# A decode step of attention and MLP: queries that wait in PSUM, a weight ring with four places, one batch's K scored inside another's softmax

## The chip, the cores and the metric

The kernel runs on one core of a Trainium2 chip. The metric is the device time of one execution in microseconds. A core has engines that run side by side: TensorE (PE in the profile, with its weight loads as PEld), VectorE (DVE), ScalarE (ACT), GpSimd (POOL) and SyncE (SP), which here issues nearly all DMA transfers. 16 DMA engines move the data from HBM to SBUF, the memory of 128 partitions on which the engines work; PSUM is the memory in which matmuls accumulate.

## The reference

Two identical layers are applied to one token of each of 8 batches, all in float32. Each layer is attention with a cache of 4096 keys, and then an MLP:

```python
def _A_ref(x, k_cache, v_cache, wq, wo):      # x: 8 x 1 x 1024
    q = (x @ wq)                              # 32 heads of 128
    k, v = each of the 4 cached heads serves 8 query heads   # 8 x 4 x 4096 x 128
    p = softmax(q . k * 128**-0.5)
    return (p . v) @ wo                       # 4096 -> 1024
def _B_ref(x, w1, b1, w2, b2):
    return gelu(x @ w1 + b1) @ w2 + b2        # 1024 -> 3584 -> 1024

x = x + _A_ref(_layernorm(x), ...)
x = x + _B_ref(_layernorm(x), ...)
x = x + _A_ref(_layernorm(x), ...)            # the same caches and weights again
x = x + _B_ref(_layernorm(x), ...)
return x
```

K and V of one batch are 8.39 MB each. Both layers read the same caches and weights.

## The kernel before

**Space.** Nearly all of SBUF is one tile, `arena`, of 216 units of 1 KB a partition. Regions A, B (named `Bb`) and C hold 64 units each, which is one batch's K or V; C's last 8 units are the first place of a ring of four places `R[0]` to `R[3]` (units 184 to 215), each for a weight tile of 1 MB. The queries of all batches (`qz`, 3 units at 200) lie in the ring's third place; the row of scores (4 units at 208) and the transposed probabilities `S` (4 units at 212) fill the fourth. So the ring has all four places only while these are not in use.

**Order of transfers.** A list `stream` holds every load in the order in which it is to be issued. `pump` issues from its head as long as the head's place is free; `give` frees a place in program order and calls `pump`. The issue itself sits in SyncE's queue and waits there until the last reader of the place is done. SyncE is in order: a load that waits holds up all behind it. The program order is written out by hand; engines run their own queues in that order.

**A layer.** `layernorm` transposes x on TensorE, subtracts the mean with further matmuls, and leaves the standard deviation to a function `variance` that is put on the list `pending`; `flush` empties that list, and is called after each step of `expand` (x times wq or w1, in two halves u = 0, 1 with eight steps each) and `project` (times wo or w2). Also the end of a half of `expand` goes to `pending`: `query_unit(u)` transposes that half's queries and copies them into `qz`, whose other columns must be zero (`open_queries` clears it on GpSimd).

**Attention.** For each batch the 8 K tiles (4 heads times 2 halves of the keys) are multiplied with the queries (`scores`), the softmax's maximum and exponential follow (`probs`), the probabilities are transposed (`turn`), and the 8 V tiles are multiplied (`values`); the end of each head pair's sum is done by `heads` a little later. A K or V tile's place is given back after its last reader.

**Between the layers.** Layer 0 goes through batches 0 to 7, layer 1 from 7 down to 0. K and V of batch 7 and K of batch 6 stay in SBUF from layer 0 to layer 1; the last tile of K of batch 6 lies in `R[0]` and is parked in PSUM meanwhile (`park`, `unpark`), so that the ring can run. The weights wo, w1, w2 of layer 0 and wq of layer 1 pass through the ring, 1 MB at a time: each tile can be loaded when the tile four before it has been multiplied. At the end of half 0 of layer 1's queries, `qz` is opened, which takes the third place out of the ring; the second half uses `R[0]`, `R[1]`, `R[3]` and the first place of region B, where K of batch 7 lies and must be scored first. That is why four K tiles of batch 7 are scored early (`early`), each behind one step of the second half. Then come, in `stream`, V of batch 6 in four pieces of 2 MB into region B, K of batch 5 in halves into region A (where V of batch 7 lies until it is multiplied) and V of batch 5 into region C. From then on each K or V of a batch is one transfer of 8.39 MB.

## Time and profile before

| | us |
|---|---|
| median of 3 runs | 881.45 (880.26 to 885.93) |
| the profiled execution | 881.5 |
| its span | 879.7 |

| in the profiled execution | |
|---|---|
| PE busy | 546.7 us, 62% of the span |
| PE weight loads | 182.9 us |
| DVE busy | 181.6 us |
| ACT busy | 47.4 us |
| read from HBM | 369.28 MB, 420 GB/s over the span |
| mean granted clock of TensorE | 0.79 |

The profile shows one execution; its times are counted from the start of the span. Layer 0's attention lasts until about 359 us, its MLP until about 468, layer 1's queries until about 513, its attention until about 781 and the rest to 877. Matmuls in float32 are recorded as two records each, so that a tile of four matmuls shows as eight. The page's share of busy time is a mean over these stages; what holds a stage up is read from that stage's own rows. In a table of stretches each row gives start and end, length, busy time of PE, weight loads, DVE, ACT and POOL with the number of instructions, the granted clock, the mean share in which the DMA engines were busy and the GB/s moved, counted where packets end.

### The profile page before, as it was taken

The numbers are of one execution on the slowest core, as the hardware profiler recorded it, in microseconds if no ns is written. First come the engines' busy times: TensorE is split into PE (matmuls) and PEld (weight loads), VectorE is DVE, ScalarE is ACT, GpSimd is POOL, SyncE is SP. The second block draws the span as 40 slices with busy tenths as digits, with TensorE's granted clock in tenths as the row PEclk, the third lists the DMA queues.
The fourth block names the chain that finished last, engine by engine and source line by source line (L and its number), as shares of the span: only waits on it lengthen the run. The fifth ranks groups of instructions, "written<-read, shape, count | busy, mean of one in ns | idle before, by whom it ended". The sixth has DMA issues, their size and how long they took to land.

```text
span 879.7 us, 8979 instructions
## 1 busy us (share of the span) xinstructions
PE 546.7 (62%) x3984; PEld 182.9 (21%) x3984; DVE 181.6 (21%) x585; ACT 47.4 (5%) x75; POOL 2.4 (0%) x13
## 2 busy tenths in 40 slices
PE   0556575555756567767667666776765655654665
PEld 0212121221212122223222122222121211222222
DVE  0002232312123232201100023333221313120110
ACT  0200000000000010000000010000000000000000
POOL 0000000000000000000000000000000000000000
PEclk9977787877777877777877879778787777777889
DMA  9999999999999999999999998999999999999997
GB/s 387 446 416 454 444 427 427 427 432 430 435 436 430 433 416 424 409 419 396 419 418 408 388 392 352 443 458 427 424 429 430 430 438 433 432 436 416 440 424 298
DMA packets 16519, 369.99 MB, mean 421 GB/s; under 512 B 1984, under 2 KB 2272, under 8 KB 2400
## 3 DMA queue, kind: packets, MB, share of 16 engines
q1 hardware_dynamic: 16336, 369.28, 98.5%
q8 instruction: 31, 0.51, 0.2%
q10 hardware_dynamic: 144, 0.13, 0.0%
q14 instruction: 8, 0.07, 0.0%
HBM read 369.28 MB, written 0.13 MB: 420 GB/s over the span
## 4 chain that ended last, share of the span: by engine, by line
DMA 68%; PE 24%; DVE 6%; issue 1%; ACT 1%; ACTq 0%; DVEq 0%; SPq 0%
DMA arena<-in_A_v_cache_dram 27%; DMA arena<-in_B_w_dram 16%; DMA arena<-in_A_k_cache_dram 16%; PE o_ps L336 7%; PE sps L280 7%; PE acc L190 4%; DMA arena<-in_A_wo_dram 4%; DMA arena<-in_A_wq_dram 3%; DVE scratch L344 3%; DMA x_row<-in_A_x_dram 3%; PE y L249 2%; PE sps L351 1%; DVE scratch L342 1%; PE sps L314 1%; DVE arena L287 1%
## 5 line engine op out<-in xcount | busy, mean ns | idle before, releaser
L280 PE MATMUL sps<-arena 128*32 128x512 f32 x992 | 140.2, 701 | 87.4 <-DMA arena<-in_A_k_cache_dram 74.0
L336 PE MATMUL o_ps<-arena 128*32 128x512 f32 x1024 | 156.8, 742 | 7.5 <-DMA arena<-in_A_v_cache_dram 7.4
L249 PE MATMUL y<-arena,oT 128*32 128x256 f32 x960 | 79.4, 477 | 53.0 <-DMA arena<-in_A_wo_dram 31.5
L190 PE MATMUL acc<-arena,xnT 128*32 128x512 f32 (+3 forms) x528 | 83.4, 716 | 44.2 <-DMA arena<-in_B_w_dram 24.0
L344 DVE SCALAR_TENSOR_TENSOR scratch<-o_ps,misc,scratch 128x128 f32<-128x128 f32 x192 | 67.3, 351 | 6.8
L280 PEld LDWEIGHTS sps<-arena 128*32 128x32 f32 x992 | 31.1, 124 | 172.8 <-DMA arena<-in_A_k_cache_dram 74.7
L314 PE MATMUL sps<-ident,arena 128*128 128x128 f32 x128 | 31.7, 393 | 43.3 <-ACT arena L303 31.4
L249 PEld LDWEIGHTS y<-arena,oT 128*32 128x32 f32 x960 | 32.0, 130 | 99.0 <-DMA arena<-in_A_wo_dram 34.6
L351 PE MATMUL sps<-misc,scratch 128*128 128x8 f32 x128 | 27.5, 288 | 33.7 <-DVE scratch L344 33.7
L287 DVE TENSOR_SCALAR_CACHE_REDUCE arena<-sps 128x512 f32<-128x512 f32 x31 | 21.4, 691 | 121.7 <-PE sps L280 121.7
L303 ACT ACTIVATE arena<-arena,bias 128x1024 f32<-128x1024 f32 x16 | 18.4, 1147 | 521.9 <-DVE scratch L300 521.9
L336 PEld LDWEIGHTS o_ps<-arena 128*32 128x32 f32 x1024 | 31.5, 129 | 70.8 <-issue 60.5
L351 PEld LDWEIGHTS sps<-misc,scratch 128*128 128x128 f32 x128 | 21.7, 213 | 105.1 <-DVE scratch L344 87.3
L342 DVE TENSOR_SCALAR scratch<-o_ps,misc 128x128 f32<-128x128 f32 x64 | 22.5, 351 | 98.2 <-PE o_ps L336 98.2
L190 PEld LDWEIGHTS acc<-arena,xnT 128*32 128x32 f32 x528 | 19.8, 127 | 92.4 <-DMA arena<-in_A_wq_dram 36.8
L353 DVE TENSOR_TENSOR oT<-sps,scratch 128x8 f32<-128x8 f32 x64 | 11.1, 173 | 111.1 <-PE sps L351 111.1
L314 PEld LDWEIGHTS sps<-ident,arena 128*128 128x128 f32 x128 | 20.2, 195 | 51.4 <-ACT arena L303 34.5
L258 DVE SCALAR_TENSOR_TENSOR x_row<-y,x_row 128x256 f32<-128x256 f32 x4 | 1.7, 425 | 110.1 <-PE y L249 110.1
L205 DVE TENSOR_SCALAR scratch<-acc,rs 128x512 f32<-128x512 f32 (+1 forms) x8 | 5.5, 684 | 81.9 <-PE acc L190 81.9
L296 PE MATMUL sps<-scratch,misc 128*128 128x128 f32 x32 | 7.8, 325 | 21.4 <-DVE scratch L292 21.4
L133 PE MATMUL sps<-ident,x_row 128*128 128x32 f32 x16 | 4.5, 373 | 25.0 <-DMA x_row<-in_A_x_dram 23.3
L319 DVE COPY arena<-sps 128x512 f32<-128x512 f32 x16 | 11.1, 691 | 40.6 <-PE sps L314 40.6
(68 smaller groups left out, 137.4 us busy)
## 6 DMA issues: line engine op xcount, KB each, us to landing
arena<-in_B_w_dram SPq DMA_DIRECT2D x29, 1024.0 KB, 8.4
arena<-in_A_wo_dram SPq DMA_DIRECT2D x16, 1024.0 KB, 8.5
arena<-in_A_wq_dram SPq DMA_DIRECT2D x16, 1024.0 KB, 8.7
arena<-in_B_w_dram SPq DMA_DIRECT2D x2, 7168.0 KB
arena<-in_A_k_cache_dram SPq DMA_DIRECT2D x3, 4096.0 KB
arena<-in_A_v_cache_dram SPq DMA_DIRECT2D x3, 4096.0 KB, 25.1
arena<-in_A_v_cache_dram SPq DMA_DIRECT2D x5, 2048.0 KB, 11.9
arena<-in_B_w_dram SPq DMA_DIRECT2D x1, 5120.0 KB
```

Of the source, the lines that this page charges most:

```text
L190: nc.tensor.matmul(acc[32 * j:32 * j + 32, lo - begins[j]:hi - begins[j]], xnT[:, kt * B:kt * B + 32], arena[:, base * KB + c + lo - a:bas ...
L249: nc.tensor.matmul(y[32 * j:32 * j + 32, 0:Q4], lhs[:, kt * B:kt * B + 32], arena[:, e:e + Q4], start=(kt == 0), stop=(kt == n_k - 1))
L280: nc.tensor.matmul(ps[32 * g:32 * g + 32, :], qz[:, c:c + 32], kt[:, g * CH:(g + 1) * CH], start=(j == 0), stop=(j == HKV - 1))
L287: nc.vector.tensor_scalar(row[:, half * CH:(half + 1) * CH], ps, SCALE, None, op0=ALU.mult, op1=ALU.max, accum_out=st["mx"][:, half:half + 1])
L303: nc.scalar.activation(row, row, AF.Exp, bias=bias, scale=1.0, accum_out=ls)
L314: nc.tensor.transpose(pp[:, t * P:(t + 1) * P], row[:, c:c + P], ident)
L319: nc.vector.tensor_copy(s[:, half], src)
L336: nc.tensor.matmul(o[32 * g:32 * g + 32, :], s[:, g], v[:, g * CH:(g + 1) * CH], start=(half == 0), stop=(half == NH - 1))
L342: nc.vector.tensor_scalar(r, o[:, 0:P], sel_t[:, 0:1], None, op0=ALU.mult)
L344: nc.vector.scalar_tensor_tensor(r, o[:, t * P:(t + 1) * P], sel_t[:, t:t + 1], r, op0=ALU.mult, op1=ALU.add)
L351: nc.tensor.matmul(po[:, 0:REP], scratch[:, a:a + DH], sel_h, start=True, stop=True)
L353: nc.vector.tensor_tensor(oT_v[:, j * REP:(j + 1) * REP, b], po[:, 0:REP], scratch[:, a + j * REP:a + (j + 1) * REP], ALU.mult)
```

## The change

It has four parts, all between layer 0's MLP and layer 1's attention but for the first.

- `layernorm` subtracts the mean with one matmul ahead of the two transposes in place of one behind each. `variance` and the other pending work are done after the second ring tile, no longer after the first (for the second half of an `expand` after the first 2048 columns, in `project` after four steps).
- The queries of half 0 of layer 1 are transposed after the first tile of half 1 and stay in PSUM; only those of batch 7 are copied, into the start of `oT` (`q7`, cleared on GpSimd after tile 3 of half 0). The early scores of batch 7 read them there. `qz` is opened and filled behind tile 6 of half 1 (tiles are counted from 0), so wq's second half uses all four ring places. The parked tile returns behind tile 4 of half 1.
- In layer 1 K of batch 6 is scored within the softmax of batch 7 (`ahead=6`): two tiles ahead of `probs`, two behind it, and four behind `turn`. Its row of scores takes a second place (`AT_ROW2`), and its first half accumulates in the pool of two buffers.
- K of batch 5 is loaded to region C, where K of batch 6 lies, and V of batch 5 to region A; the later homes swap A and C accordingly, and the pieces of layer 1's w2 lie in A and B.

```diff
-AT_QZ, AT_ROW, AT_S = 200, 208, 212
+AT_QZ, AT_ROW, AT_S, AT_ROW2 = 200, 208, 212, 203
...
     def layernorm(xr, rsum):
         pt = small_ps("pt")
+        nc.tensor.matmul(pt[:, 0:8 * B], rsum.to_broadcast([P, P]), nmean[:, 0:B].unsqueeze(1).to_broadcast([P, 8, B]), start=True, stop=False)
         for i in range(2):
-            o = pt[:, i * 4 * B:(i + 1) * 4 * B]
-            nc.tensor.matmul(o, xr[:, i * P:(i + 1) * P], ident.rearrange("p (j q) -> p j q", j=4)[:, :, 0:B], start=True, stop=False)
-            nc.tensor.matmul(o, rsum.to_broadcast([P, P]), nmean[:, 0:B].unsqueeze(1).to_broadcast([P, 4, B]), start=False, stop=True)
+            nc.tensor.matmul(pt[:, i * 4 * B:(i + 1) * 4 * B], xr[:, i * P:(i + 1) * P],
+                             ident.rearrange("p (j q) -> p j q", j=4)[:, :, 0:B], start=False, stop=(i == 1))
...
-                    flush()
+                    if at >= (2 - u) * W:
+                        flush()
...
+    q7 = oT[:, 0:Q_AT[1] + PAD]
+
+    def query_unit_late(u):
+        src = turned(2 * REP)
+        if u == 1:
+            put_queries(1, src)
+            return
+        for e in range(2):
+            nc.vector.tensor_copy(q7[:, Q_AT[e]:Q_AT[e] + REP], src[:, e * REP:(e + 1) * REP, B - 1])
+        st["q0"] = src
+
+    def open_queries_late():
+        open_queries()
+        put_queries(0, st.pop("q0"))
...
-                flush()
+                if kt >= 4:
+                    flush()
...
+        for b in order:
+            score(b)
+            nxt = ahead if b == order[0] else None
+            if nxt is not None:
+                score(nxt, 2)
             probs(b)
+            if nxt is not None:
+                score(nxt, 2)
             turn(b)
+            if nxt is not None:
+                score(nxt)
...
-    weights("q1", wq, [ring[0:8], [(e, TILE) for e in (R[0], R[1], R[3], Bb) * 2]])
-    cache(1, v_keys(6), vc[6], [(Bb + 32, 2), (Bb, 2), (Bb + 16, 2), (Bb + 48, 2)])
-    cache(1, k_keys(5), kc[5], [(A, 4), (A + 32, 4)])
-    cache(1, v_keys(5), vc[5], [(C, 4), (C + 32, 4)])
+    weights("q1", wq, [ring[0:8], ring[0:8]])
+    cache(1, v_keys(6), vc[6], [(Bb, 2), (Bb + 32, 2), (Bb + 16, 2), (Bb + 48, 2)])
+    cache(1, k_keys(5), kc[5], [(C, 4), (C + 32, 4)])
+    cache(1, v_keys(5), vc[5], [(A, 4), (A + 32, 4)])
...
-    weights("p1", w2, [[(C, 40), (C + 40, 28), (C + 68, 20), (Bb, 12), (Bb + 12, 8), (Bb + 20, 4)]])
+    weights("p1", w2, [[(A, 40), (A + 40, 28), (A + 68, 20), (A + 88, 12), (A + 100, 8), (A + 108, 4)]])
...
     def early(key):
-        scores(key, spare=key[3] == 1)
+        scores(key, spare=key[3] == 1, late=True)
         give(pieces[key], TILE)
...
-            expand("q1", W, rs, query_unit, {(0, "end"): open_queries} | {(1, i): (lambda key=key: early(key)) for i, key in enumerate(first)})
+            expand("q1", W, rs, query_unit_late, {(0, 3): clear, (1, 4): unpark, (1, 6): open_queries_late}
+                   | {(1, i): (lambda key=key: early(key)) for i, key in zip((1, 2, 3, 5), first)})
             flush()
-            last = attention(range(B)[::-1], set(), done=first, after={7: unpark})
+            last = attention(range(B)[::-1], set(), done=first, ahead=6)
```

How the rows stand in TensorE's queue, from the end of layer 0 on. Before, the start of layer 1 (L133 and L134 transpose x and subtract the mean, L127 spreads a sum, L190 are the tiles of wq, L217 transposes queries, L280 scores a K tile with four rows):

```order
L133 MATMUL sps<-ident,x_row 128x32
L134 MATMUL sps<-nmean,rsum 128x32
L133 MATMUL sps<-ident,x_row 128x32
L134 MATMUL sps<-nmean,rsum 128x32
L127 MATMUL sps<-rsum,nmean 32x1 x4
L190 MATMUL acc<-arena,xnT 32x512 x4
L127 MATMUL sps<-ss,nmean 32x1 x4
L190 MATMUL acc<-arena,xnT 32x512 x32
L217 MATMUL sps<-ident,scratch 128x128 x4
L280 MATMUL sps<-arena 32x512 x4
L190 MATMUL acc<-arena,xnT 32x512 x4
L280 MATMUL sps<-arena 32x512 x4
```

The same place in the changed kernel (the lines are now L134, L132, L128, L191, L219 and L301):

```order
L132 MATMUL sps<-nmean,rsum 128x64
L134 MATMUL sps<-ident,x_row 128x32 x2
L128 MATMUL sps<-rsum,nmean 32x1 x4
L191 MATMUL acc<-arena,xnT 32x512 x8
L128 MATMUL sps<-ss,nmean 32x1 x4
L191 MATMUL acc<-arena,xnT 32x512 x28
L219 MATMUL sps<-ident,scratch 128x128 x4
L191 MATMUL acc<-arena,xnT 32x512 x4
L301 MATMUL sps<-arena,oT 32x512 x4
L191 MATMUL acc<-arena,xnT 32x512 x4
L301 MATMUL sps<-arena,oT 32x512 x4
```

One matmul fewer stands ahead of the first tile, the variance stands behind two tiles instead of one, and the first early score behind the second tile of half 1 instead of the first, reading its queries from `oT`.

Before, from the last query transposes to the first V tiles of batch 7 (L296 is the maximum's matmul, L314 turns the probabilities, L321 their sum, L336 a V tile's rows):

```order
L217 MATMUL sps<-ident,scratch 128x128 x4
L280 MATMUL sps<-arena 32x512 x8
L280 MATMUL s_ps<-arena 32x512 x8
L296 MATMUL sps<-scratch,misc 128x128
L314 MATMUL sps<-ident,arena 128x128 x8
L321 MATMUL sps<-scratch,misc 128x32
L336 MATMUL o_ps<-arena 32x512 x12
```

And in the changed kernel (L318, L336, L343 and L358 for these):

```order
L219 MATMUL sps<-ident,scratch 128x128 x4
L301 MATMUL sps<-arena 32x512 x8
L301 MATMUL s_ps<-arena 32x512 x16
L318 MATMUL sps<-scratch,misc 128x128
L301 MATMUL s_ps<-arena 32x512 x8
L336 MATMUL sps<-ident,arena 128x128 x8
L343 MATMUL sps<-scratch,misc 128x32
L301 MATMUL sps<-arena 32x512 x16
L358 MATMUL o_ps<-arena 32x512 x12
```

The 32 rows of batch 6's K, which came behind batch 7's V, now stand in three groups around batch 7's softmax; the V tiles of batch 7 come behind all of them. SyncE's queue holds the same transfers in the same order as before, into other places.

More of the change, by code (lines that the diff above doesn't have):

```diff
@@ L111, in open_queries @@
         nc.gpsimd.memset(qz, 0.0)
+    st = {}
     pending = []
@@ L301, in probs @@
         ls = small.tile([P, 1], F32, name="ls")
-        row = place(AT_ROW, 4)
+        row = place(rows[b], 4)
         nc.scalar.activation(row, row, AF.Exp, bias=bias, scale=1.0, accum_out=ls)
@@ L306, in turn @@
     def turn(b):
-        row = place(AT_ROW, 4)
+        row = place(rows[b], 4)
         take(AT_S, 4, "S")
@@ L354, in heads, with attention, score @@
                                 scratch[:, a + j * REP:a + (j + 1) * REP], ALU.mult)
-    def attention(order, keep, done=(), after={}):
-        for b in order:
-            for key in k_keys(b):
-                if key in done:
-                    continue
-                scores(key)
+    def attention(order, keep, done=(), after={}, ahead=None):
+        scored = set(done)
+        def score(b, n=NR):
+            for key in [e for e in k_keys(b) if e not in scored][:n]:
+                scored.add(key)
+                scores(key, spare=b == ahead and key[3] == 0)
                 while ready:
```

33 lines of the change are left out of this document (19 added, 14 removed).

## The prediction

> **What bounds the kernel now.** I read the page's slices in time and its DMA part first, then the chain of waits, then tables of stretches, then the SyncE queue's issues.
>
> ```profile
> DMA  9999999999999999999999998999999999999997
> GB/s 387 446 416 454 444 427 427 427 432 430 435 436 430 433 416 424 409 419 396 419 418 408 388 392 352 443 458 427 424 429 430 430 438 433 432 436 416 440 424 298
> q1 hardware_dynamic: 16336, 369.28, 98.5%
> DMA 68%; PE 24%; DVE 6%; issue 1%; ACT 1%; ACTq 0%; DVEq 0%; SPq 0%
> ```
>
> The DMA engines are busy nearly everywhere and the chain that ended last is 68% DMA. So the time is 369.28 MB over the rate, plus the stretches in which the engines starve. The GB/s digits dip in slices 23 to 25 (22 us each). The table of stretches shows where; its last three columns are granted clock, DMA share and GB/s.
>
> ```profile
> 398.00:412.00 14.00, 10.42 (x74) 4.79 (x74) 0.97 (x4) 2.14 (x4) 0.00 (x0) 0.73 0.96 379
> 412.00:466.00 54.00, 36.11 (x310) 12.18 (x310) 4.81 (x16) 1.88 (x3) 0.00 (x0) 0.78 1.01 419
> 473.00:482.00 9.00, 6.07 (x48) 1.11 (x44) 0.16 (x1) 0.62 (x2) 0.00 (x0) 0.77 1.00 391
> 490.00:496.00 6.00, 4.44 (x38) 1.24 (x30) 0.47 (x2) 0.00 (x0) 0.00 (x0) 0.94 0.82 287
> 512.00:515.00 3.00, 2.27 (x20) 0.96 (x24) 0.73 (x3) 0.00 (x0) 0.00 (x0) 1.00 0.88 300
> 516.00:528.00 12.00, 7.21 (x40) 2.84 (x36) 4.07 (x13) 2.75 (x4) 0.00 (x0) 0.73 1.02 406
> 528.00:534.00 6.00, 4.54 (x40) 1.50 (x36) 3.16 (x10) 0.00 (x0) 0.00 (x0) 0.97 0.39 128
> 545.00:600.00 55.00, 39.52 (x264) 13.48 (x260) 19.14 (x62) 3.67 (x6) 0.00 (x0) 0.81 1.01 437
> 600.00:860.00 260.00, 159.08 (x1224) 56.38 (x1216) 55.80 (x182) 13.21 (x22) 0.00 (x0) 0.78 1.00 432
> ```
>
> Three full rates can be read: 419 with the ring's 1 MB tiles, 406 with V of batch 6 (2 MB pieces, share 1.02), 432 with K and V in larger pieces. Against them five stretches fall short: 398 to 412, 473 to 482, 490 to 496, 512 to 515 and 528 to 534. From 545 to 860 the DMA never lacks work, so a microsecond of transfer won before 545 is a microsecond at the end, as long as no new gap opens.
>
> Who holds the transfers back? SyncE issues in order; these are its issues around the gaps (start, duration, what).
>
> ```profile
> 482.96 0.33 SPq L163 DMA_DIRECT2D arena<-in_A_wq_dram  x1
> 488.80 0.33 SPq L163 DMA_DIRECT2D arena<-in_A_wq_dram  x1
> 493.31 0.33 SPq L163 DMA_DIRECT2D arena<-in_A_wq_dram  x1
> 501.43 0.33 SPq L163 DMA_DIRECT2D arena<-in_A_v_cache_dram  x1
> 511.50 0.33 SPq L163 DMA_DIRECT2D arena<-in_A_v_cache_dram  x1
> 517.09 0.33 SPq L163 DMA_DIRECT2D arena<-in_A_v_cache_dram  x1
> 531.33 0.33 SPq L163 DMA_DIRECT2D arena<-in_A_k_cache_dram  x1
> 537.36 0.33 SPq L163 DMA_DIRECT2D arena<-in_A_k_cache_dram  x1
> 567.37 0.33 SPq L163 DMA_DIRECT2D arena<-in_A_k_cache_dram  x1
> ```
>
> After the tile issued at 482.96 the next two went out 5.8 and 4.5 us later, though a tile takes about 2.5 us to transfer: the ring had lost a place to the queries, and the 493.31 one waited for a first score. The second piece of V of batch 6 waited until 511.50, and K of batch 5 until 531.33, 14.2 us after the piece before it, because its place held V of batch 7. The chain over that time names what ran meanwhile:
>
> ```profile
> 500.57 8.95 DMA arena<-in_A_wq_dram
> 509.57 1.92 PE acc L190 x8
> 513.38 1.92 PE sps L280 x16
> 515.31 1.76 PE s_ps L280 x16
> 524.67 3.62 PE o_ps L336 x16
> ```
>
> The last wq tile lands at 500.57 + 8.95 = 509.52, the queries are ready at 513.38 (3.9 us later), batch 7's four remaining K tiles take 1.92 + 1.76 = 3.7 us, and the softmax, 7.6 us, fills 517.07 to 524.67 before the first V tile is multiplied.
>
> **The change part by part.**
>
> *Ring with four places, queries of half one held in PSUM.* The tiles no longer wait for the query place or for scores, so they follow one another at the ring's own spacing:
>
> ```profile
> 484.33 1.93 PE L190 MATMUL acc<-arena,xnT 128*32 128x512 f32 x8 [1.42 <-DMA arena<-in_A_wq_dram]
> 489.30 1.76 PE L190 MATMUL acc<-arena,xnT 128*32 128x512 f32 x8 [0.55 <-DMA arena<-in_A_wq_dram]
> ```
>
> Two tiles later is 4.97 us, so 2.485 each. Tile 8 (the first of half two) is taken at 489.30; seven more put the last tile at 489.3 + 17.4 = 506.7 instead of 509.52. As lost rate, the 490 to 496 gap is 6 × (1 − 287/419) = 1.9 us, and it should go whole. PE must keep pace: a tile's eight records and a score's eight take 0.96 us each where the clock is granted (half of the 1.92 for sixteen above), 1.92 together against 2.485; where it is not, 1.93 each (the row at 484.33), and a backlog grows by 1.4 us a tile. V of batch 6 goes to the place whose first two K tiles are scored behind tiles 9 and 10, so its first two issues stand ready before the ring ends: the 512 to 515 gap, 3 × (1 − 300/406) = 0.8 us, goes too.
>
> What is added there: one more clearing on GpSimd and one that moves behind tile 14, plus two small copies.
>
> ```profile
> 486.37 0.68 POOL L111 MEMSET arena<- 128x704 f32 x1 [484.03 <-PE acc L190]
> ```
>
> The moved clearing costs 0.68 us, and VectorE stands behind it with two copies before it may evict the second half. Cover: tile 15 lands 2.485 us after tile 14 and takes 1.9. So I cost it at nothing; without cover, 0.7 to 1.2 us on the queries, against the slack below. The parked tile's return (ScalarE and VectorE) moves behind tile 12, where neither has other work. The clearing of the short query copy is queued five tiles ahead of its first reader.
>
> *K of batch 6 scored inside batch 7's softmax, K of batch 5 into its place.* With L = 506.7 for the last tile, queries are ready at 510.6, batch 7 is scored at 514.3, two K tiles of batch 6 (1.9 us) at 516.2, the maximum's matmul, then two more at about 518.6. There the first half of K of batch 5 can be issued. The DMA is then still busy with V of batch 6: 8.39 MB at 406 is 20.7 us, until 527.4. So the issue comes 8.8 us before it is needed. The rest of the softmax, now done at 524.67 with queries at 513.38, would be done near 522 to 523.5; with the last four K tiles (3.7 us) behind it the second half is issued near 527, needed at 537.1. V of batch 7 starts there; its halves go out after 531.33 − 524.67 = 6.7 and 12.7 us, near 533.7 and 539.8, needed at 546.8 and 556.5. K of batch 4 needs all of V of batch 6 multiplied: 539.8 + 7.6 of softmax + 12.7 = 560.1, needed at 566.2. The smallest slack on this path is these 6.1 us. The 528 to 534 gap, 6 × (1 − 128/432) = 4.2 us, goes. Against that, packets that were under way in the gap's ramp are counted after it: 545 to 600 ran at 437, which gives back 55 × (437/432 − 1) = 0.6.
>
> Together 1.9 + 0.8 + 4.2 − 0.6 = 6.3. A second way counts when the transfer of K of batch 5 begins. Behind its issue at 531.33 the engines stay empty for a while:
>
> ```profile
> 531.40:532.20 0.80, 0.72 (x8) 0.00 (x0) 0.73 (x3) 0.00 (x0) 0.00 (x0) 1.00 0.00 0
> ```
>
> So it begins no earlier than 532.2 now, and at 527.4 with the change: 4.8, and the ramp behind it, of which no row gives the size, comes on top. I take 6.1, nearer the first way since that counts bytes (4.8 to 6.9).
>
> *Layernorm with three matmuls, variance behind the second tile, the flush in the projection behind the second.* The start of the first MLP shows what it holds up.
>
> ```profile
> 398.27 0.61 PE L134 MATMUL sps<-nmean,rsum 128*128 128x32 f32 x2
> 398.70 0.61 PE L133 MATMUL sps<-ident,x_row 128*128 128x32 f32 x2
> 400.06 1.92 PE L190 MATMUL acc<-arena,xnT 128*32 128x512 f32 x8
> 401.35 0.69 PE L127 MATMUL sps<-ss,nmean 128*32 128x1 f32 x8
> 397.33 0.33 SPq L163 DMA_DIRECT2D arena<-in_B_w_dram  x1
> 402.96 0.33 SPq L163 DMA_DIRECT2D arena<-in_B_w_dram  x1
> ```
>
> One matmul fewer is 398.70 − 398.27 = 0.43 us; the variance matmuls take 0.69 out of the first tile. So the first place comes free 1.1 us earlier than 402.96. The loss there is 14 × (1 − 379/419) = 1.3 us; I take 1.1. At the start of the second layer the loss is 9 × (1 − 391/419) = 0.6, and I take half of it, 0.3, since the one matmul fewer is the same but I have no row in which the variance delays a tile there. The first and the last layernorm stand behind transfers of many MB, and the projection's flush delays half a tile at most: nothing, inside the bounds of 0 to 1.9 for all.
>
> *Homes swapped between regions A and C.* K and V only trade places, but the second piece of the last w2 now needs space that the first half of the last MLP must free.
>
> ```profile
> 830.46 45.35 DMA arena<-in_B_w_dram
> ```
>
> This last transfer is issued at 830.46 and lands 45.4 us later; 72 of the matrix's 112 KB a partition, 9.4 MB or 21.8 us at 432, make up the second piece and what follows, so the second piece is needed near 854. By 830 that half has been read: nothing, with some 20 us of cover.
>
> **Sum.** The profiled execution took 881.5 us, its span 879.7; the median of the runs is 881.45, so they agree. 881.5 − 6.1 − 1.1 − 0.3 = 874.0. With the bounds, 6.9 + 1.9 gives 872.7, and 4.8 + 0 gives 876.7.
>
> **The rivals.** About 1% is what a measurement of this kernel can tell from no change: under 872.6 is faster, over 890.3 slower.
>
> *More goes than I count.* The dips inside V of batch 6 are late starts too, and the pieces run at 419: 8.39 MB in 20.0 us, 0.7 better. With the upper bounds, 881.5 − 6.9 − 1.9 − 0.7 = 872.0. For it: its pieces were issued at 511.50 and 517.09, with the engines low before each. Against: the share is 1.02 at 406. 16%.
>
> *A gap takes the gap's place.* The queries come later than 510.6, because VectorE waits behind the clearing, or PE falls behind the ring at half clock; tiles of batch 7 then free V's third piece late. With two pieces at 5.2 us ahead of it and 0.9 from issue to start (531.33 to 532.2) it must be out by 506.7 + 10.3 − 0.9 = 516.1, and I expect 512.5: 3.6 us of slack. Two half-clock stretches on this path would use it up and cost some 2 to 4 us: 877. 11%.
>
> *Slower, by the clock.* PE's order now has K of batch 6 ahead of V of batch 7, and everything up to K of batch 4 is one chain on PE with 6.1 us of slack. The clock decides:
>
> ```profile
> 528.00:548.00 20.00, 14.83 (x125) 4.42 (x118) 8.15 (x26) 0.00 (x0) 0.00 (x0) 0.99 0.85 353
> 548.00:559.00 11.00, 7.50 (x36) 3.05 (x36) 2.42 (x8) 1.84 (x3) 0.00 (x0) 0.54 0.99 427
> ```
>
> At half clock eight records take 1.93 us, as at 484.33, against 0.96: twice. In the first of these stretches PE is busy 14.83 of 20 us; of the 49.5 us from 510.6 to 560.1 that makes some 37 of PE work. If half clock held for all of it, K of batch 4 would come 37 us later, 31 beyond the slack, and the end near 905; it is slower than before from 6.1 + 7.5 = 13.6 us on, that is when over a third of that work runs at half clock beyond what the rows already hold. Against it: the busier stretch above was granted 0.99 for 20 us and only the next 11 were at 0.54. [...] 4%.
>
> *It does not do what it says.* The share of 98.5% leaves no room: the memory gives about 420 on the mean whatever is queued, a shortfall is made up later in any case, as the 437 behind the gap hints, and the end stays at 881. Against: 437 over 55 us returns only 0.6 us, and 432 was held for 260 us. [...] 4%.
>
> **How the numbers follow.** My forecast, 874.0, has 65%, its own range 872.7 to 876.7. Faster by over 1% takes the first rival, whole, and a little of the forecast's lower tail: 0.20. Slower takes the clock rival: 0.04. The rest, 0.76, is within 1%. For eight in ten the range takes the first rival and most of the second, with half a microsecond for the scatter of the runs at the lower end: 871.6 to 878.0.
>
> **What would show it.** Right: stretches 490 to 515 at 406 or more, no stretch of 6 us below 390 between 485 and 545, the first half of K of batch 5 issued before 522, the last wq tile taken near 506.7, and 398 to 412 at 405 or more. Wrong: SyncE waiting on scores or on V of batch 7 with the DMA share under 0.9 anywhere from 500 to 600; K of batch 4 issued after 567; PE's clock at 0.5 for over 15 us in a row; or the gaps closed and the rate from 545 to 860 under 432.

## The result and the profile after

The changed kernel takes 874.03 us (median, 873.39 to 875.50); the kernel before, run beside it, 883.68 us (880.26 to 885.93). The ratio is 0.9896, with a 95% interval of 0.9854 to 0.9939: 1.0% faster. The predicted time was 874.0. The profiled execution of the changed kernel took 875.5 us, its span is 873.7, 6.0 us less than that of before.

The ratio's interval allows anything from 0.6 to 1.5%. The GB/s of the changed kernel's page, in the slices with which the prediction began:

```profile
GB/s 389 433 435 433 432 433 433 432 433 436 438 436 436 438 401 426 405 399 384 422 422 421 421 411 434 434 433 433 432 436 445 433 441 430 432 430 417 443 415 302
```

The dip in slices 23 to 25 (388, 392, 352 before) is gone. Another stayed, around slices 17 to 19. The stretches of the changed kernel show both (last three columns: granted clock, DMA share, GB/s):

```profile
397.00:411.00 14.00, 11.12 (x87) 4.50 (x88) 1.41 (x6) 2.15 (x4) 0.00 (x0) 0.74 0.97 367
490.00:515.00 25.00, 19.27 (x124) 5.05 (x124) 3.91 (x9) 2.31 (x2) 0.69 (x1) 0.77 1.02 425
512.00:518.00 6.00, 6.00 (x36) 1.68 (x40) 0.70 (x2) 0.00 (x0) 0.00 (x0) 0.58 0.93 363
485.00:545.00 60.00, 44.97 (x305) 13.16 (x306) 16.04 (x50) 5.98 (x8) 0.69 (x1) 0.82 1.00 421
600.00:860.00 260.00, 160.05 (x1226) 57.86 (x1226) 54.28 (x178) 13.21 (x22) 0.00 (x0) 0.76 1.00 430
```

From 485 to 545 the DMA moves 421 GB/s, with a short remainder of a dip from 512 to 518. The start of the first MLP (397 to 411, 367) is no better than before (398 to 412, 379). From 545 to 860 the rate is 432, against 433 before.

Where the time went is best read from landings on the chain of waits. Before, the last wo tile and the last w2 tile of layer 0 (start, duration, what; the landing is the sum):

```profile
387.42 7.87 DMA arena<-in_A_wo_dram
458.72 7.90 DMA arena<-in_B_w_dram
```

After, the same two, then the last wq tile and the last transfer of all:

```profile
389.20 7.72 DMA arena<-in_A_wo_dram
460.35 7.89 DMA arena<-in_B_w_dram
499.77 8.59 DMA arena<-in_A_wq_dram
828.09 41.75 DMA arena<-in_B_w_dram
```

| landing | before | after | after less before |
|---|---|---|---|
| last wo tile, layer 0 | 395.29 | 396.92 | +1.63 |
| last w2 tile, layer 0 | 466.62 | 468.24 | +1.62 |
| last wq tile, layer 1 | 509.52 | 508.36 | −1.16 |
| last transfer | 875.81 | 869.84 | −5.97 |

The changed kernel's profiled execution arrives 1.6 us late at the first place where the change acts on the ring. Across layer 0's MLP it gains nothing, across layer 1's queries 2.8 us, and behind them 4.8 us. So the change is worth 7.6 us in these two executions, all of it behind the last w2 tile of layer 0. The medians differ by more, 9.65 us. The profiled execution of before, 881.5, is one of its faster ones: of the 51 executions of before that stand beside the runs of this document, 12 took 881.5 or less and 31 over 883. Only that one has a trace, so where the others lose their 2 us and more is open.

SyncE's issues in the changed kernel, for V of batch 6 (third piece), K of batch 5 (two halves), V of batch 5 (first half) and K of batch 4:

```profile
515.66 0.33 SPq L164 DMA_DIRECT2D arena<-in_A_v_cache_dram  x1
522.14 0.33 SPq L164 DMA_DIRECT2D arena<-in_A_k_cache_dram  x1
528.94 0.33 SPq L164 DMA_DIRECT2D arena<-in_A_k_cache_dram  x1
533.68 0.33 SPq L164 DMA_DIRECT2D arena<-in_A_v_cache_dram  x1
560.59 0.33 SPq L164 DMA_DIRECT2D arena<-in_A_k_cache_dram  x1
```

K of batch 5 leaves at 522.14 in place of 531.33, with V of batch 6 still under way. And the chain over the softmax of batch 7:

```profile
508.41 1.11 PE acc L191 x8
511.96 3.64 PE sps L301 x16
515.61 4.20 PE s_ps L301 x32
520.23 1.85 PE s_ps L301 x16
525.31 3.57 PE sps L301 x32
528.88 1.76 PE o_ps L358 x16
```

TensorE goes from score to score. The first two K tiles took 3.64 us where they took 1.92 before: TensorE's clock was near half there (0.58 from 512 to 518), and the third piece of V of batch 6, which waits for these scores, left late.

### The profile page after: what moved, and what is told of

Same layout as the page of the kernel before. It is cut to its first block, busy times and chain, and to the rows that moved or that the text cites. A ratio compares the mean times of both kernels' runs of the same rounds, so it can differ in the third digit from the quotient of the medians.

```text
span 873.7 us, 8968 instructions
## 1 busy us (share of the span) xinstructions
PE 545.9 (62%) x3976; PEld 181.0 (21%) x3976; DVE 181.9 (21%) x587; ACT 47.5 (5%) x75; POOL 2.6 (0%) x14
## 4 chain that ended last, share of the span: by engine, by line
DMA 67%; PE 24%; DVE 6%; issue 1%; ACT 1%; SPq 0%; ACTq 0%; DVEq 0%
DMA arena<-in_A_v_cache_dram 22%; DMA arena<-in_A_k_cache_dram 20%; DMA arena<-in_B_w_dram 17%; PE o_ps L358 7%; PE sps L301 7%; PE acc L191 4%; DMA arena<-in_A_wo_dram 4%; DVE scratch L366 3%; DMA arena<-in_A_wq_dram 3%; DMA x_row<-in_A_x_dram 3%; PE y L268 2%; PE sps L373 2%; DVE scratch L364 1%; PE sps L336 1%; DVE arena L309 1%
## 5 line engine op out<-in xcount | busy, mean ns | idle before, releaser
L301 PE MATMUL sps<-arena 128*32 128x512 f32 x944 | 135.2, 711 | 89.1 <-DMA arena<-in_A_k_cache_dram 77.0
L358 PE MATMUL o_ps<-arena 128*32 128x512 f32 x1024 | 154.3, 731 | 8.2 <-DMA arena<-in_A_v_cache_dram 8.1
L268 PE MATMUL y<-arena,oT 128*32 128x256 f32 x960 | 83.6, 497 | 50.8 <-DMA arena<-in_A_wo_dram 30.4
L191 PE MATMUL acc<-arena,xnT 128*32 128x512 f32 (+3 forms) x528 | 81.0, 689 | 42.2 <-DMA arena<-in_B_w_dram 22.7
L301 PEld LDWEIGHTS sps<-arena 128*32 128x32 f32 x944 | 29.8, 124 | 171.4 <-DMA arena<-in_A_k_cache_dram 76.1
L336 PE MATMUL sps<-ident,arena 128*128 128x128 f32 x128 | 30.9, 386 | 42.3 <-ACT arena L325 30.4
L358 PEld LDWEIGHTS o_ps<-arena 128*32 128x32 f32 x1024 | 30.9, 127 | 69.3 <-issue 58.3
L191 PEld LDWEIGHTS acc<-arena,xnT 128*32 128x32 f32 x528 | 19.6, 123 | 89.9 <-DMA arena<-in_A_wq_dram 34.9
L336 PEld LDWEIGHTS sps<-ident,arena 128*128 128x128 f32 x128 | 19.6, 190 | 51.1 <-ACT arena L325 34.2
L318 PE MATMUL sps<-scratch,misc 128*128 128x128 f32 x32 | 7.8, 326 | 18.7 <-DVE scratch L314 18.7
L132 PE MATMUL sps<-nmean,rsum 128*128 128x64 f32 x8 | 2.2, 374 | 25.4 <-DVE rsum L467 23.7
L343 PE MATMUL sps<-scratch,misc 128*128 128x32 f32 x32 | 10.0, 404 | 12.5 <-DVE arena L341 12.5
```

What stands on the lines that cost most here:

```text
L191: nc.tensor.matmul(acc[32 * j:32 * j + 32, lo - begins[j]:hi - begins[j]], xnT[:, kt * B:kt * B + 32], arena[:, base * KB + c + lo - a:bas ...
L268: nc.tensor.matmul(y[32 * j:32 * j + 32, 0:Q4], lhs[:, kt * B:kt * B + 32], arena[:, e:e + Q4], start=(kt == 0), stop=(kt == n_k - 1))
L301: nc.tensor.matmul(ps[32 * g:32 * g + 32, :], q[:, c:c + 32], kt[:, g * CH:(g + 1) * CH], start=(j == 0), stop=(j == HKV - 1))
L336: nc.tensor.transpose(pp[:, t * P:(t + 1) * P], row[:, c:c + P], ident)
L358: nc.tensor.matmul(o[32 * g:32 * g + 32, :], s[:, g], v[:, g * CH:(g + 1) * CH], start=(half == 0), stop=(half == NH - 1))
```

## The experiments

Theory: the time is the volume over the rate plus the gaps in the transfers; each gap is a place that SyncE waits for, and the change closes those at the end of the ring (2.8 us) and before K of batch 5 (4 to 5 us). Rivals: the gap only moves; TensorE's chain bounds the stage; the layernorm and the flush carry a part of it.

### The layernorm and the flush alone

The kernel before with these two edits of the change, nothing else.

```diff
+        nc.tensor.matmul(pt[:, 0:8 * B], rsum.to_broadcast([P, P]), nmean[:, 0:B].unsqueeze(1).to_broadcast([P, 8, B]), start=True, stop=False)
         for i in range(2):
...
-            nc.tensor.matmul(o, rsum.to_broadcast([P, P]), nmean[:, 0:B].unsqueeze(1).to_broadcast([P, 4, B]), start=False, stop=True)
...
-                    flush()
+                    if at >= (2 - u) * W:
+                        flush()
...
-                flush()
+                if kt >= 4:
+                    flush()
...
```

> The kernel before with the layernorm of three matmuls and the later flush alone. By the prediction's sum 1.1 + 0.3 = 1.4 us less than before (ratio 0.9984): the first place of the ring at the start of the first MLP is given back some 1.1 us earlier after the last wo tile, and the last w2 tile of layer 0 lands 71.2 - 1.1 = 70.1 us after the last wo tile in place of 71.3. By the rival reading, in which the two profiled executions of before and after both show 71.3 us from the last wo tile to the last w2 tile, the ring runs dry there for the time that x needs and a short lead at its first tile is lost again: 0 us there, 0 to 0.6 at the start of layer 1.

883.14 us against 884.12 of before, ratio 0.9999 (0.9981 to 1.0017). The first two issues of the MLP's ring tiles, of this kernel, and the start of its first tile on the chain of waits:

```profile
397.31 0.33 SPq L163 DMA_DIRECT2D arena<-in_B_w_dram  x1
402.42 0.33 SPq L163 DMA_DIRECT2D arena<-in_B_w_dram  x1
399.62 3.63 PE acc L190 x13
```

The first place comes free 5.11 us after the last wo tile's, against 402.96 − 397.33 = 5.63 before: 0.5 us, half of what the prediction took, with TensorE's clock at 0.50 from 397 to 403 in both. The tile's matmuls start 0.44 us earlier (399.62 against 400.06), which is the one matmul fewer (0.43); only some 0.1 is left for the variance, which the prediction had at 0.69. The last w2 tile lands 70.7 us behind the last wo tile, between the two that were expected. The time shows no gain, but its interval also holds the 0.9984 of the sum, so this run alone does not settle it.

### All but the layernorm and the flush

The changed kernel with these two edits undone.

```diff
-        nc.tensor.matmul(pt[:, 0:8 * B], rsum.to_broadcast([P, P]), nmean[:, 0:B].unsqueeze(1).to_broadcast([P, 8, B]), start=True, stop=False)
         for i in range(2):
...
+            nc.tensor.matmul(o, rsum.to_broadcast([P, P]), nmean[:, 0:B].unsqueeze(1).to_broadcast([P, 4, B]), start=False, stop=True)
...
-                    if at >= (2 - u) * W:
-                        flush()
+                    flush()
...
-                if kt >= 4:
-                    flush()
+                flush()
...
```

> The changed kernel with the layernorm of four matmuls and the flush of before. By the prediction's sum it is 1.4 us slower than the changed kernel (ratio to before 0.992 to 0.993), and the first ring place of the first MLP comes free 1.1 us later. By the rival reading it is as fast as the changed kernel within 0.6 us, the stretch from the last wo tile to the last w2 tile 71.3 us in both.

873.09 us (872.47 to 873.26), ratio 0.9876 (0.9861 to 0.9891): not slower than the changed kernel, and outside the 0.992 to 0.993 that the sum asked for. And a surprise, in the 14 us at the start of the first MLP of this kernel and in its first two issues there:

```profile
398.00:412.00 14.00, 9.31 (x86) 3.44 (x85) 0.95 (x4) 2.15 (x4) 0.00 (x0) 1.00 1.01 420
397.29 0.33 SPq L164 DMA_DIRECT2D arena<-in_B_w_dram  x1
400.75 0.33 SPq L164 DMA_DIRECT2D arena<-in_B_w_dram  x1
```

With the old layernorm the first place is free after 3.46 us and there is no gap at all, at 420 GB/s. What differs is the clock: 1.00 here, against 0.73 before and 0.74 in the changed kernel over such a stretch. The stretch from the last wo to the last w2 tile, expected as 71.3 us in both, is 69.7 us here. This gave a new theory, tested below: the granted clock, and not the order of the matmuls, decides whether the ring runs dry at a layernorm.

### The ring and the queries alone

The changed kernel without K of batch 6 in the softmax, with the homes, layernorm and flush of before.

```diff
-            last = attention(range(B)[::-1], set(), done=first, ahead=6)
+            last = attention(range(B)[::-1], set(), done=first)
...
-    cache(1, k_keys(5), kc[5], [(C, 4), (C + 32, 4)])
-    cache(1, v_keys(5), vc[5], [(A, 4), (A + 32, 4)])
+    cache(1, k_keys(5), kc[5], [(A, 4), (A + 32, 4)])
+    cache(1, v_keys(5), vc[5], [(C, 4), (C + 32, 4)])
...
```

> The kernel before with the ring of four places, the queries held in PSUM, the parked tile's early return and V of batch 6 into the first place first; K of batch 6 is scored after V of batch 7, and the homes, the layernorm and the flush are those of before. By the theory that every transfer held back counts: the last wq tile lands 2.5 to 2.9 us earlier relative to the last w2 tile (40.0 to 40.4 us behind it in place of 42.9), the softmax moves with it, and K of batch 5 is issued 2.8 us earlier too; 2.5 to 3 us less than before, ratio near 0.997. The gap before K of batch 5 stays at 2 us or more. By the rival that the queue behind evens it out: no change of the time, since K of batch 5 is still waited for.

879.98 us, ratio 0.9953 (0.9935 to 0.9971): 4.1 us less, somewhat more than expected. A stretch over the ring's end and one over the gap before K of batch 5, and SyncE's issues for K of batch 5:

```profile
486.00:500.00 14.00, 11.22 (x80) 2.23 (x76) 0.99 (x3) 0.00 (x0) 0.00 (x0) 0.82 1.01 425
526.00:532.00 6.00, 4.51 (x40) 1.43 (x36) 3.12 (x11) 0.00 (x0) 0.00 (x0) 1.00 0.50 175
528.36 6.37 SPq L164 DMA_DIRECT2D arena<-in_A_k_cache_dram  x2
```

The ring's gap is gone (425 GB/s), the other stays (175), and K of batch 5 is issued 3.0 us earlier than before: the whole softmax has moved with the last wq tile. The rival that the queue evens it out falls.

### K of batch 6 in the softmax and the homes alone

The changed kernel with the ring, the queries, the layernorm and the flush of before.

```diff
-    weights("q1", wq, [ring[0:8], ring[0:8]])
+    weights("q1", wq, [ring[0:8], [(e, TILE) for e in (R[0], R[1], R[3], Bb) * 2]])
...
-            expand("q1", W, rs, query_unit_late, {(0, 3): clear, (1, 4): unpark, (1, 6): open_queries_late}
-                   | {(1, i): (lambda key=key: early(key)) for i, key in zip((1, 2, 3, 5), first)})
+            expand("q1", W, rs, query_unit, {(0, "end"): open_queries} | {(1, i): (lambda key=key: early(key)) for i, key in enumerate(first)})
...
-            last = attention(range(B)[::-1], set(), done=first, ahead=6)
+            last = attention(range(B)[::-1], set(), done=first, ahead=6, after={7: unpark})
```

> The kernel before with K of batch 6 scored inside the softmax of batch 7 and the swapped homes alone; ring, layernorm and flush are those of before. By the theory: the last wq tile lands as before (42.9 us behind the last w2 tile), the gap of 3.5 to 5 us before K of batch 5 goes, its first half is issued near 524 in place of 531.3: 3.6 to 4.8 us less than before, ratio near 0.995. By the rival that the gap only moves to V of batch 5 or K of batch 4, since V of batch 7 comes later on TensorE: under 1.5 us less.

877.17 us, ratio 0.9924 (0.9906 to 0.9943): 7 us less, more than expected. The ring's end and the time of the other gap, then the issues for K of batch 5:

```profile
488.00:498.00 10.00, 7.85 (x56) 1.85 (x52) 1.23 (x3) 0.00 (x0) 0.00 (x0) 0.82 0.90 333
524.00:536.00 12.00, 9.75 (x84) 3.54 (x84) 6.07 (x17) 1.51 (x2) 0.00 (x0) 1.00 1.02 437
523.99 7.13 SPq L164 DMA_DIRECT2D arena<-in_A_k_cache_dram  x2
```

Now the ring's gap stays (333) and the second is gone (437). The two halves of the change add up: 0.47% and 0.76% make 1.23%, and both together without the layernorm gave 1.24%.

Both medians gained more than expected; the median of before beside them, 884.1, is 2.6 above the profiled execution of before. Counted within each profiled execution, from the landing of the last w2 tile of layer 0 to that of the last transfer, the gains are near the theory's. These are the two, first for the ring and the queries, then for this kernel:

```profile
458.86 7.97 DMA arena<-in_B_w_dram
827.34 45.35 DMA arena<-in_B_w_dram
```

```profile
459.48 7.90 DMA arena<-in_B_w_dram
830.58 41.60 DMA arena<-in_B_w_dram
```

It is 409.2 us before, 405.9 with the ring and the queries, 404.8 here and 401.6 in the changed kernel (401.4 to 401.8 in five further profiles that have both halves): 3.3 and 4.4 make 7.7, and 7.6 was measured.

### The order on TensorE without, and the homes without

Two kernels that keep one of the two things on which the second gap rests. First the new homes with K of batch 6 scored behind V of batch 7:

```diff
-            last = attention(range(B)[::-1], set(), done=first, ahead=6)
+            last = attention(range(B)[::-1], set(), done=first)
```

> The changed kernel, but K of batch 6 is scored behind V of batch 7 again, while K of batch 5 keeps its new place, where K of batch 6 lies. By the theory that SyncE's wait for that place decides: V of batch 7 starts near 523.5, is done near 536, the first half of K of batch 6 near 540, and only there K of batch 5 can be issued; V of batch 6 has landed by 527.4, so the DMA engines stand for some 13 us, and the time is about 13 us above the changed kernel's (near 887, ratio to before about 1.003). By the rival that the new order on TensorE is of no matter and the ring alone made the gain: within 2 us of the changed kernel.

889.56 us, ratio 1.0074 (1.005 to 1.0097): slower than before, some 15 us above the changed kernel (13.0 by the spans of the profiled executions, 886.7 and 873.7). The transfers and the issue:

```profile
527.00:539.00 12.00, 9.01 (x78) 2.61 (x70) 5.33 (x16) 0.00 (x0) 0.00 (x0) 1.00 0.00 1
538.40 4.79 SPq L164 DMA_DIRECT2D arena<-in_A_k_cache_dram  x2
```

For these 12 us the DMA engines stand still, until the first half of K of batch 6 has been scored. Then the new order with the old homes:

```diff
-    cache(1, k_keys(5), kc[5], [(C, 4), (C + 32, 4)])
-    cache(1, v_keys(5), vc[5], [(A, 4), (A + 32, 4)])
+    cache(1, k_keys(5), kc[5], [(A, 4), (A + 32, 4)])
+    cache(1, v_keys(5), vc[5], [(C, 4), (C + 32, 4)])
...
```

> The changed kernel with the homes of before: K of batch 6 is scored inside the softmax of batch 7, but K of batch 5 goes to the place of V of batch 7 and V of batch 5 to that of K of batch 6. By the theory K of batch 5 is issued when half of V of batch 7 is multiplied, near 533.7, and V of batch 6 has landed by 527.4: a gap of some 7 us, 6 to 7 us above the changed kernel (near 881, ratio about 0.997). By the rival that the scores in the softmax make the gain by themselves: within 2 us of the changed kernel.

880.92 us, ratio 0.9972 (0.9952 to 0.9991), 7 us above the changed kernel. K of batch 5 is issued at 531.13, when half of V of batch 7 has been multiplied:

```profile
526.00:532.00 6.00, 5.15 (x46) 1.36 (x38) 3.51 (x12) 0.00 (x0) 0.00 (x0) 1.00 0.01 3
531.13 6.36 SPq L164 DMA_DIRECT2D arena<-in_A_k_cache_dram  x2
```

So the order and the homes are worth their gain only together: the old homes leave nothing of it (0.9972, against 0.9953 for the ring and the queries), and the new homes without the order lose.

### More work for TensorE on the path

The changed kernel with 5 or 14 more matmuls, whose result is not used, between the last scores of batch 6 and V of batch 7 (the diff shows the first; the second has 14 in place of 5).

```diff
+        ahead_of = B - 1 if ahead is not None else None
...
+            if b == ahead_of:
+                pd = small_ps("pt")
+                for _ in range(5):
+                    nc.tensor.matmul(pd, ident, place(AT_S, 2), start=True, stop=True)
             for key in v_keys(b):
```

> The changed kernel with 5 more matmuls of 128x512 on TensorE (4 to 6 us, their result is not used) between the last scores of batch 6 and V of batch 7. By the theory K of batch 4, issued at 560.6 and needed at 566.5 (the end of V of batch 5 at 567.4 less 0.9), has 5.9 us of slack, so it costs nothing: within 1 us of the changed kernel. By the rival that TensorE's chain bounds this stage: 4 to 6 us slower.

> The changed kernel with 14 such matmuls at the same place (12 to 15 us). By the theory the slack of 5.9 us is used up and the rest shows: 6 to 10 us above the changed kernel (880 to 884), with a gap in the transfers before K of batch 4 and none before. By the rival that TensorE's chain bounds the stage: 12 to 15 us; by the rival that the slack is larger, since TensorE catches up between: under 3 us.

With five (4.56 us) 874.43 us, ratio 0.9898 (0.9868 to 0.9927): nothing. With fourteen 880.73 us, ratio 0.9964 (0.9945 to 0.9983): 6.7 us. The added matmuls of the second, the transfers up to 555 and around the issue of K of batch 4, and that issue:

```profile
523.97 12.28 PE L409 MATMUL sps<-arena,ident 128*128 128x512 f32 x28
515.00:555.00 40.00, 31.62 (x174) 12.82 (x178) 10.99 (x37) 3.68 (x6) 0.00 (x0) 0.93 1.01 433
563.00:570.00 7.00, 4.67 (x41) 1.52 (x37) 3.90 (x13) 0.00 (x0) 0.00 (x0) 1.00 0.44 154
568.33 0.33 SPq L164 DMA_DIRECT2D arena<-in_A_k_cache_dram  x1
```

12.28 less the slack of 5.9 us is 6.4, and 6.7 was measured at the medians (5.9 us more than the changed kernel from the last w2 tile to the last transfer). TensorE's chain does not bound the stage; the slack before K of batch 4 is real and about as long as predicted (6.1).

### The clock at a layernorm, and a fifth place for V

The changed kernel again, with two additions, one by one and together. One keeps TensorE busy while it waits for wo and w2 tiles of layer 0; the other puts one tile of V of batch 6 into a ring place that is free by then.

```diff
                 if c + step == n_kb:
                     give(base, n_kb)
+                    if name in ("o0", "p0") and kt < n_k:
+                        pd = small_ps("s")
+                        nc.tensor.matmul(pd, ident, place(AT_A, 2), start=True, stop=True)
...
-    cache(1, v_keys(6), vc[6], [(Bb, 2), (Bb + 32, 2), (Bb + 16, 2), (Bb + 48, 2)])
+    cache(1, v_keys(6), vc[6], [(Bb, 2), (Bb + 32, 2), (R[1], 1), (Bb + 16, 2), (Bb + 48, 1)])
```

> The changed kernel once more, beside the three below: 874.0, ratio to before 0.988 to 0.991. At the start of the first MLP the first ring place comes free 5.1 us after x's last matmul when TensorE's clock is granted at half there, and 3.2 us after it when it is granted whole; which of the two happens is not set by the kernel.

> The changed kernel with one more matmul of 128x512 (0.88 us at full clock, its result is not used) behind each tile of wo and w2 in layer 0, in time in which TensorE waits for the next tile. By the theory that the granted clock, and not the number of matmuls, decides whether the ring runs dry at a layernorm: the clock is 1.0 in the 8 us behind x at both starts, the first place of the first MLP comes free 3.2 us after x's last matmul, the 14 us there run at 415 GB/s or more; 0.5 to 1.6 us less than the changed kernel. By the rival that the order of the layernorm's matmuls decides: no change; if the clock stays low under the added work, 0 to 1 us slower.

> The changed kernel with one tile of V of batch 6 put into the second ring place, which nobody uses after wq: five tiles of V can be issued before batch 7's last K tiles are scored instead of four. By the theory that the third piece, issued at 515.66 when the transfers before it were nearly done, leaves a dip (512 to 518 at 363 GB/s): that dip goes, 0.5 to 1 us less than the changed kernel. By the rival that the smaller pieces cost what the dip did: no change.

> Both of these: 1 to 2.5 us less than the changed kernel, near 872, ratio to before 0.986 to 0.988. By the rivals: as the changed kernel.

| kernel | median (range), us | ratio to before (95%) |
|---|---|---|
| changed kernel again | 873.93 (872.10 to 874.63) | 0.9901 (0.9873 to 0.9928) |
| with added matmuls | 872.35 (871.98 to 873.69) | 0.9890 (0.9863 to 0.9917) |
| with a fifth place | 873.28 (872.04 to 874.37) | 0.9895 (0.9868 to 0.9923) |
| with both | 872.19 (872.04 to 872.44) | 0.9885 (0.9856 to 0.9915) |

The start of the first MLP, first of the changed kernel again, then of the one with added matmuls, each with its first two issues there:

```profile
398.00:412.00 14.00, 10.54 (x84) 4.52 (x84) 1.07 (x6) 2.15 (x4) 0.00 (x0) 0.82 0.98 379
397.00:403.00 6.00, 5.34 (x40) 2.54 (x33) 1.24 (x5) 1.88 (x3) 0.00 (x0) 0.50 1.01 421
397.65 0.33 SPq L164 DMA_DIRECT2D arena<-in_B_w_dram  x1
402.75 0.33 SPq L164 DMA_DIRECT2D arena<-in_B_w_dram  x1
```

```profile
397.00:411.00 14.00, 8.96 (x83) 3.65 (x84) 0.95 (x4) 2.15 (x4) 0.00 (x0) 1.00 1.01 420
396.47 0.33 SPq L164 DMA_DIRECT2D arena<-in_B_w_dram  x1
399.65 0.33 SPq L164 DMA_DIRECT2D arena<-in_B_w_dram  x1
```

In the profile with more work TensorE was granted its whole clock (1.00 from 397 to 411), the first place came free after 3.18 us, and the gap closed: 420 against 379 GB/s over 14 us is 1.4 us, and the medians differ by 1.6, though the intervals overlap. At the start of the second layer, where the clock was expected whole as well, it was 0.76 from 466 to 474; no gap came there either (423 GB/s from 473 to 482). The added work is not needed for that. The kernel with five more matmuls in layer 1's softmax runs the changed kernel's own program up to there, and in its profile the whole clock was granted with nothing added at this place:

```profile
397.00:403.00 6.00, 4.06 (x46) 2.01 (x42) 1.38 (x6) 2.15 (x4) 0.00 (x0) 1.00 1.01 418
397.12 0.33 SPq L164 DMA_DIRECT2D arena<-in_B_w_dram  x1
400.29 0.33 SPq L164 DMA_DIRECT2D arena<-in_B_w_dram  x1
```

The kernel without the early scores shows the same. So the profiles have the old and the new layernorm each at both clocks; this is the time from the issue behind the last wo tile to the next, when the first place is free:

| us until the first place is free | clock 0.50 from 397 to 403 | clock 1.00 |
|---|---|---|
| old layernorm and flush | 5.63 (before) | 3.46 (all but the layernorm) |
| new layernorm and flush | 5.10 (changed kernel, both profiles) | 3.17 (five more matmuls; without the early scores) |

The clock is worth 1.9 to 2.2 us, the layernorm 0.3 to 0.5. In all fourteen profiles, nine had a clock of 0.50 to 0.57 from 397 to 403 and moved 365 to 392 GB/s from 398 to 412; five had 1.00 and moved 420 to 422, among them one with the old layernorm. So it is the clock that decides here, not the order of the matmuls. The fifth place gives 0.65 us at the medians, within the intervals. Whether the dip from 512 to 518 comes at all went with the clock, too: the changed kernel's second profile had none without the fifth place:

```profile
512.00:518.00 6.00, 6.00 (x58) 1.97 (x50) 2.33 (x9) 0.92 (x1) 0.00 (x0) 1.00 1.01 431
```

431 GB/s at a clock of 1.00, where the first profile had 363 at 0.58. K of batch 5 was issued at 518.39 there, not at 522.14:

```profile
518.39 7.13 SPq L164 DMA_DIRECT2D arena<-in_A_k_cache_dram  x2
```

Of the fifth place alone nothing can be said. The version with both has the lowest median, 872.19 us, within the interval of the others, and its six runs lie within 0.4 us.

## Why the prediction was right, and where it was not

- **What bounds the kernel.** Right: transfers, with the gaps before 545. A gap opened on purpose (12 us in the kernel without the early scores) came out at the end in full (13.0 by the spans), and work for TensorE came out only beyond its slack (4.56 us cost nothing, 12.28 cost 6.7).
- **The ring's end.** Foreseen at 506.7 for the last wq tile; 508.36 less the 1.6 us by which this execution came late is 506.7. The sum's 1.9, with the 0.3 of the layernorm there, is 2.2; 2.8 was measured. The changed kernel's second profile has 2.5, so the excess is within what differs from one execution to the next.
- **V of batch 6.** The third piece was foreseen at 512.5, 514.1 with the 1.6, and left at 515.66, since two K tiles took 3.64 us at half clock. That is the rival of a gap in the gap's place, in part: as lost rate it is 6 × (1 − 363/420) = 0.8 us in the profiled execution, and none in another one. At the end it does not show: the profile with the dip takes 401.6 us from the last w2 tile to the last transfer, the one without it 401.8, and 545 to 600 ran at 444 GB/s in the first, 435 in the second. So a short dip there was made up, which the prediction's "a microsecond at the end" did not allow for; what makes it up is not shown.
- **K of batch 5 and the 528 to 534 gap.** Foreseen at 518.6 (520.2 with the 1.6); 522.14. It was late for the mark "before 522", but the cover of 8.8 us took it; where the clock was whole it left at 518.39. The terms 0.8 + 4.2 − 0.6 make 4.4; 4.8 was measured. Together with the ring that is 7.6 against the 6.4 that I took. The lower of the two ways of counting, which missed the ramp, had drawn the value down by 0.2. The rest is of the size of the term that the first rival names: 406 GB/s was taken as the full rate of V of batch 6, which ran at 431 in the changed kernel's second profile, and 8.39 MB take 1.2 us less at that. This is argued from the rates, no run isolates it.
- **K of batch 4.** Foreseen at 560.1 (561.7), issued at 560.59; the slack of 6.1 us is confirmed by the added matmuls. The slower case by the clock did not come: 0.82 over 485 to 545, and from 485 to 860 half clock was granted for some 10 us in a row at most.
- **The layernorm: wrong.** The step that failed is "So the first place comes free 1.1 us earlier", and behind it "I take 1.1". It is 0.5 us: before, the variance's matmuls (401.35 to 402.04) ended with the tile's own (401.98) and delayed the place by some 0.1, not by their 0.69. And the 1.3 us of loss were put down to the work ahead of the tiles, where the clock decides: at half clock, with less work, the gap stayed (367 and 379), at whole clock, with the old order, it was gone (420). Measured across that MLP: 0. The 0.3 for the start of the second layer fares no better: with the new layernorm 473 to 482 moved 418 GB/s where the clock was 0.80 from 466 to 474, and 375 where it was 0.50, against 391 at 0.55 before.
- **The sum.** The step of 7.5 us agrees with the 7.6 of the two profiles because the layernorm's 1.1 too much and the gaps' 1.2 too little nearly cancel. It is less than the 9.65 of the medians: the 881.5 from which I reckoned lay 2.2 below the median of before, and the step fell short by as much. That the median agrees with 874.0 to a tenth is luck on both counts.
- **The marks.** Held: 425 from 490 to 515, and the last wq tile. Missed in the profiled execution: 512 to 518 (363), K of batch 5 (522.14), 398 to 412 (365); all three came with a low clock there (0.58 from 512 to 518, 0.50 from 397 to 403). Of the marks for wrong, the rate from 545 to 860 is 432, at the edge of "under 432" and 1 below before. Half clock for over 15 us in a row came once, from 364 to 380, ahead of the places at which the change was to gain. The others did not come.
- **The chances.** "Within 1%" had 0.76, and the measured 1.04% lies just beyond; its interval, 0.6 to 1.5%, covers both sides. The spread of before, 880 to 886, should have told that one profiled execution need not stand for its median (883.7 to 884.1 in the later runs).
- **The rate.** The rival by which the memory gives about 420 on the mean whatever is queued, and the end stays at 881, did not come: the mean over the span is 423 GB/s against 420 before, 600 to 860 moved 430 against 432, and the last transfer landed 5.97 us earlier.

## What to carry to other kernels

Where transfers bound the time, look for the places that the issuing queue waits for, and ask for each what is the last reader and when it could be done; reordering the readers and choosing which place is reloaded first belong together, and here one without the other gained nothing (0.9972, against 0.9953 for the ring and the queries) or lost (1.0074). Check then how much slack each later issue has: here 4.6 us more work on TensorE cost nothing and 12.3 cost 6.7. And a gap whose length depends on TensorE's speed should be judged with its granted clock beside it, in more than one profile.

## What the hardware showed that was not expected

TensorE's granted clock at one place of the same program differs from run to run, and a gap in the transfers with it: 363 GB/s at 0.58 and 431 at 1.00 for the changed kernel from 512 to 518; 365 to 392 at 0.50 to 0.57 and 420 to 422 at 1.00 at the start of the first MLP. With useless work for TensorE in its waits (one matmul a tile, recorded with 1.1 us) the clock was 1.00 from 380 to 411, against 0.70 and 0.60 from 380 to 397 in the changed kernel's two profiles. That the work raises the clock is not shown by this: the kernel with five more matmuls in layer 1's softmax had 1.00 from 397 to 403 with nothing added there.

Whether the clock makes the scatter of the times is open. With the added matmuls and the fifth place six runs lay within 0.4 us, against 2.5 for the changed kernel beside it and 7 for the one before; but with the added matmuls alone they lay 1.7 apart, at mean clocks of 0.818 to 0.824. The mean clock of every execution is known. Over the ten of the changed kernel the time falls as it rises, from 875.5 at 0.785 to 872.1 at 0.806; over those of the kernel before it hardly does (correlation −0.3 for 47).
